# Score matmuls over both batches of a K pair, a mask matmul, and one matmul to turn P, in a two-layer decode kernel

## The chip, the cores and the metric

The kernel runs on one core of a Trainium2 chip. The metric is device time in microseconds, as the median of several runs; lower is better. A core has five engines that run their own instruction streams and meet at semaphores: TensorE (PE, matmuls; its weight loads appear as PEld), VectorE (DVE), ScalarE (ACT), GpSimd (POOL) and SyncE (SP, which here only issues transfers). Matmuls write to PSUM, eight banks of 512 float32 columns on 128 partitions; everything else lies in SBUF.

## What is computed

Two layers of a decode step for four sequences of one token each, with the same weights and the same K and V caches in both layers:

```python
x = x + attn(layernorm(x))    # wq, K cache, V cache, wo
x = x + glu(layernorm(x))     # wg, wu, wd
x = x + attn(layernorm(x))
x = x + glu(layernorm(x))
# attn: q = x @ wq                                  32 query heads, 8 KV heads, Dh = 128
#       scores = q . k * Dh**-0.5  over the last 2048 cached keys
#       o = softmax(scores) @ v;  return o @ wo
# glu:  (sigmoid(x @ wg) * (x @ wu)) @ wd            D = 512, F = 1792
```

There are B = 4 batches; four query heads share one KV head (REP = 4). Everything is bf16 with float32 sums.

## The kernel before

**Loads.** K of all eight KV heads stays in SBUF: it is loaded once, in the first layer, into slots of its own. A K pair (`load_k`, line 432) is the K of one head for two batches, 1 MB: partition 2p + i holds 32 consecutive keys of batch i of the pair, p = 0 to 63. V, wo, wq, wg, wu and wd go through a pool of nine 1 MB tiles (`_SlotPool`), which grows in the second layer, when a head's K is no longer needed. V is loaded in the same pair layout, once in each layer; one V tile is stashed in PSUM banks 0 to 3 between the layers. All loads are issued by SP in one order (line 385); a load that needs a tile waits until the last reader of that tile is done.

**Order of the work.** The program is a list of operations with what they read and write. `_schedule` (line 86) simulates it with rough costs (`_TM`, line 263) and picks the order of each engine's instructions; `_assign_sync` puts in the waits. An engine then runs its list strictly in that order. An operation's cost in the list is therefore no time, but it can change the order.

**Attention.** A unit is one KV head in one layer; there are eight in each layer. `attn` (line 829) keeps two units in flight, in buffers k2 = 0 and 1: the scores and statistics of unit u + 2 come before P times V of unit u, and the turning of P of unit u + 2 comes after it.

- `k_transpose` (line 685, first layer only): four 32x32-block transposes on DVE, each over 128 x 1024 float32, in place. Afterwards a partition is (block a of 32 old partitions, pair of head dimensions), and along the partition lie j (key within the old partition), c (half of the head), k = 2x + i (old partition within the block: x, and batch i of the pair) and t (even or odd dimension).
- `q_unit` (line 669): q of the unit's four heads is spread by four small matmuls into a block form, so that a matmul over 128 partitions gives the four blocks a separate rows; ACT copies it to `qbd`.
- `softmax_unit` (line 694): the scores are sixteen matmuls (line 708). For each cp = (c, t), four, and each batch b, four, the weights are 16 columns (a, query head r) of `qbd` and the moving operand is 512 keys of batch b alone, (j 32, x 16): every second k, four bf16 elements (8 bytes) apart. The four batches go to four column tiles, 32 partitions apart in one PSUM bank; 16 of each 32 rows are written. DVE then takes the maximum over 512 columns (line 716), adds a mask and the row maximum (`mk`, line 719), and takes the negated maximum over the four blocks by a transposing reduction (line 722). ACT computes exp with that as bias and sums each row (line 725), into the single buffer `prow`.
- `turn_p` (line 731): four matmuls with the permutation `perm` bring P's rows to their places for P times V: 64 rows of P at a time, 256 columns each, into two PSUM banks (line 737). ACT copies both banks to `prow`, interleaving them (line 742); DVE transposes 32x32 blocks into `ebuf` (line 746). The row sums are split in three bf16 parts on POOL (lines 750 to 754), summed over partitions by three matmuls (line 760) and inverted (line 767).
- `pv_unit` (line 770): for each V tile, 32 matmuls with 128 x 128 of V as weights and 8 columns of P (line 781), then normalization (line 789), a permutation (line 799) and a masking (line 804); `wo_unit` (line 811): 16 matmuls with wo (line 820).

**Setup.** `perm`, `sel_f`, `sel_b`, `sel_r` and `maskr` (lines 522 to 560) are built once on POOL and DVE. The two score banks are zeroed once (line 521), and the part of a bank that unit 8 uses instead, since the stash fills bank 0, is zeroed by `zero_q` (line 664). Query projections are at lines 629 to 665, the GLU at 865 to 977.

## Time and profile before

Seven runs: median 188.09 us, 187.28 to 189.4. The profile is of one further execution.

| | |
|---|---|
| profiled execution, its own time | 188.77 us |
| its span | 186.9 us |
| PE busy | 111.5 us (60%), 2016 matmuls |
| PE weight loads busy | 62.1 us (33%), 2016 |
| DVE busy | 90.5 us (48%), 209 |
| ACT busy | 31.2 us (17%) |
| POOL busy | 15.2 us (8%) |
| DMA | 72.12 MB, mean 386 GB/s |
| mean granted clock of PE | 0.708 |
| score matmuls, line 708 | 256, 32.3 us busy, mean 632 ns |
| turn of P, line 737 | 64, 7.1 us busy, mean 305 ns |
| copy of turned P, line 742 | 16, 9.4 us, mean 586 ns |
| row maximum, line 716 | 16, 10.9 us, mean 683 ns |

Where the stages lie: first projection to 15 us, first attention to 107, first GLU to 119, second projection to 130, second attention 126 to 175, last GLU to 186.

How to read it: busy times add up what an engine spent in instructions, while matmuls overlap (four column tiles run side by side), so PE's busy time is not a measure of its rate. A group's row gives its line, engine, operation, output and inputs with shapes, count, busy time and mean, and then the idle time just before it with what ended most of that. "issue" stands for time in which the engine waited for nothing that the profile shows. The granted clock is 0.50 or 1.00 of full speed in any moment.

### The profile page before, as it was taken

To read this page: it belongs to the slowest core of one execution; us is meant where nothing else is said; L and a number is where in the kernel's file an instruction comes from. 1 tells how busy PE (TensorE), PEld (TensorE's weight loads), DVE (VectorE), ACT (ScalarE), POOL (GpSimd) and SP (SyncE) were. 2 spreads that over 40 slices of the span, in tenths; PEclk is the share of its full clock that TensorE was granted. 3 is DMA by queue.
4 is the path that set the end of the run, shared out by engine and by line. 5 is a ranking of instruction groups with operands and counts; after the bars stand their busy time and mean duration, and the time that the engine had idled before them with its cause. 6 is when DMAs were issued, how large, how long until landed. Compare 5 with 4: busy or idle time off the path is not lost.

```text
span 186.9 us, 4539 instructions
## 1 busy us (share of the span) xinstructions
PE 111.5 (60%) x2016; PEld 62.1 (33%) x2016; DVE 90.5 (48%) x209; ACT 31.2 (17%) x78; POOL 15.2 (8%) x79
## 2 busy tenths in 40 slices
PE   1544541744637164460855474449989989985685
PEld 0011110332404133040435332212255655485342
DVE  6209998355763838539322542226634442340340
ACT  2002011510303003020020010001364211320010
POOL 5000010210101001010010000000113110110000
PEclk9999998755857655585575555555998796785557
DMA  5999999999999999999999999999999999999800
GB/s 199 422 422 431 421 415 416 426 417 419 413 423 419 421 422 411 420 421 421 414 417 419 401 406 414 370 375 421 363 401 428 424 415 419 415 404 411 323 32 1
DMA packets 12307, 72.12 MB, mean 386 GB/s; under 512 B 1144, under 2 KB 1152, under 8 KB 5632
## 3 DMA queue, kind: packets, MB, share of 16 engines
q1 hardware_dynamic: 12280, 71.84, 94.0%
q8 instruction: 15, 0.25, 0.5%
q14 instruction: 4, 0.03, 0.0%
q10 hardware_dynamic: 8, 0.00, 0.0%
HBM read 71.83 MB, written 0.00 MB: 384 GB/s over the span
## 4 chain that ended last, share of the span: by engine, by line
DMA 47%; PE 31%; DVE 8%; SPq 6%; issue 3%; ACT 2%; ACTq 0%
DMA arena<-in_A_v_cache_dram 24%; DMA arena<-in_A_k_cache_dram 14%; PE ps L708 10%; PE ps L781 8%; SPq L385 6%; DMA arena<-in_A_wq_dram 5%; DMA arena<-in_B_w_up_dram 5%; DVE arena L689 2%; PE ps L882 2%; PE ps L820 2%; PE ps L737 2%; PE ps L940 2%; PE ps L641 2%; DVE ps L494 1%; DVE nmax L716 1%
## 5 line engine op out<-in xcount | busy, mean ns | idle before, releaser
L781 PE MATMUL ps<-ebuf,arena 128*128 128x8 bf16 x1024 | 31.6, 167 | 21.7 <-DMA arena<-in_A_v_cache_dram 18.4
L708 PE MATMUL ps<-arena,qbd 128*16 128x512 bf16 x256 | 32.3, 632 | 17.7 <-DVE arena L689 17.3
L689 DVE STREAM_TRANSPOSE arena<-arena 128x1024 f32<-128x1024 f32 x32 | 37.8, 1215 | 1.7 <-DMA arena<-in_A_k_cache_dram 1.3
L781 PEld LDWEIGHTS ps<-ebuf,arena 128*128 128x128 bf16 x1024 | 28.8, 100 | 28.4 <-DMA arena<-in_A_v_cache_dram 24.4
L716 DVE TENSOR_REDUCE nmax<-ps 128x1 f32<-128x512 f32 x16 | 10.9, 683 | 23.4 <-PE ps L708 23.4
L725 ACT ACTIVATE prow<-ps,nmax 128x512 bf16<-128x512 f32 x16 | 11.0, 687 | 42.6 <-DVE nmax L722 29.4
L708 PEld LDWEIGHTS ps<-arena,qbd 128*16 128x16 bf16 x256 | 6.3, 99 | 31.0 <-DVE arena L689 17.9
L750 POOL CAST s<-psm 128x1 bf16<-128x1 f32 x16 | 3.0, 187 | 146.0 <-ACT prow L725 146.0
L682 ACT CAST qbd<-ps 128x256 bf16<-128x256 f32 x16 | 6.0, 372 | 42.9 <-PE ps L708 34.0
L641 PE MATMUL ps<-arena,xn 128*4 128x512 bf16 x64 | 8.3, 601 | 8.1 <-DMA arena<-in_A_wq_dram 8.1
L789 DVE TENSOR_TENSOR onb<-ps,rinv 128x16 bf16<-128x16 f32 x16 | 2.9, 182 | 20.3 <-PE ps L781 20.3
L742 ACT CAST prow<-ps 128x512 bf16<-128x512 f32 x16 | 9.4, 586 | 10.2 <-PE ps L737 10.0
L746 DVE STREAM_TRANSPOSE ebuf<-prow 128x256 f32<-128x256 f32 x16 | 7.0, 436 | 7.5 <-ACT prow L742 7.5
L820 PE MATMUL ps<-onp,arena 128*128 128x16 bf16 x256 | 9.3, 173 | 1.8 <-DVE onp L804 1.0
L820 PEld LDWEIGHTS ps<-onp,arena 128*128 128x128 bf16 x256 | 7.9, 101 | 4.4 <-issue 3.6
L618 ACT ACTIVATE lnv<-ps 128x4 f32<-128x4 f32 x4 | 0.7, 174 | 51.2 <-PE ps L614 51.2
L652 DVE STREAM_TRANSPOSE ebuf<-ps 128x512 f32<-128x512 f32 x4 | 2.9, 717 | 12.9 <-PE ps L641 12.8
L737 PE MATMUL ps<-prow,perm 64*128 64x256 bf16 x64 | 7.1, 305 | 3.1 <-ACT prow L725 3.1
L882 PE MATMUL ps<-arena,xn 128*4 128x448 bf16 x64 | 6.8, 564 | 2.4 <-DMA arena<-in_B_w_up_dram 1.7
L677 PE MATMUL ps<-qh,eyew 32*128 32x64 bf16 x64 | 5.6, 216 | 3.4 <-ACT qbd L682 1.9
L677 PEld LDWEIGHTS ps<-qh,eyew 32*128 32x128 bf16 x64 | 3.3, 105 | 9.3 <-ACT qbd L682 4.0
L804 DVE TENSOR_TENSOR onp<-ps,maskp 128x64 bf16<-128x64 f32 x16 | 3.5, 220 | 5.9 <-PE ps L799 5.8
(71 smaller groups left out, 85.9 us busy)
## 6 DMA issues: line engine op xcount, KB each, us to landing
arena<-in_A_v_cache_dram SPq DMA_DIRECT2D x30, 1024.0 KB, 20.9
arena<-in_A_k_cache_dram SPq DMA_DIRECT2D x16, 1024.0 KB, 25.0
arena<-in_A_wq_dram SPq DMA_DIRECT2D x8, 1024.0 KB, 9.1
arena<-in_A_wo_dram SPq DMA_DIRECT2D x4, 1024.0 KB, 25.5
arena<-in_B_w_gate_dram SPq DMA_DIRECT2D x4, 896.0 KB, 18.0
arena<-in_B_w_up_dram SPq DMA_DIRECT2D x4, 896.0 KB, 16.1
arena<-in_B_w_down_dram SPq DMA_DIRECT2D x2, 1024.0 KB, 13.2
arena<-in_B_w_down_dram SPq DMA_DIRECT2D x1, 768.0 KB, 7.4
```

The lines of the kernel that those rows point to most:

```text
L385: o = P.op("sync", name, 0.0, lambda e, dst=dst, src=src: e.dma_start(dst, src), r=r, w=w, dma_bytes=nbytes, dma_rate=tm[rate])
L641: last = pe.matmul(ps[32 * hh:32 * hh + NB, qb, :], xn[:, c * NB:(c + 1) * NB], tile_ap(s)[:, o + hh * 512:o + (hh + 1) * 512], start=(c = ...
L677: last = pe.matmul(dst[:, :, :, a * REP:(a + 1) * REP], eyew[32 * hh:32 * hh + 32, 96 - 32 * a:224 - 32 * a], src, start=True, stop=True)
L689: P.op("vector", "T%d_%d" % (h, t), c_dve(1024), lambda v, v32=v32: v.transpose(v32, v32), r=[("slot", 4 * h + t)], w=[("slot", 4 * h + t)])
L708: last = pe.matmul(ps[32 * gi:32 * gi + NR, bank, :], qbd[:, q0:q0 + NR], kt[:, cp // 2, cp % 2, b % 2, :, :], start=(cp == 0), stop=(cp = ...
L716: lambda v: v.tensor_reduce(nmax[:, k2:k2 + 1], ps[:, bank, :], AXX, ALU.max),
L725: lambda a: a.activation(prow[:, :].rearrange("p (m x t) -> p m x t", x=16, t=2), ps[:, bank, :].rearrange("p (m t x) -> p m x t", x=16, t ...
L737: last = pe.matmul(ps[:, PBS[i], 0:256], perm[64 * i:64 * i + 64, jh * 128:(jh + 1) * 128], prow[64 * i:64 * i + 64, jh * 256:(jh + 1) * 2 ...
L742: lambda a: a.copy(prow[:, :].rearrange("p (y i t) -> p i y t", i=2, t=2), ps[:, PBS[0]:PBS[0] + 2, 0:256].rearrange("p i (y t) -> p i y t ...
L781: last = pe.matmul(ps[:, ob, bp * 8:bp * 8 + 8], src[:, j * 128:(j + 1) * 128], ev[:, j % 2, j % 16 // 2, x0:x0 + 8], start=(j == 0), stop ...
L820: last = pe.matmul(ps[:, WB, c * NR:(c + 1) * NR], tile_ap(s)[:, o + r_ * D + c * 128:o + r_ * D + (c + 1) * 128], ov[:, r_ * NR:(r_ + 1) ...
L882: last = pe.matmul(ps[32 * g:32 * g + NB, OBS[n], 0:NF], xn[:, c * NB:(c + 1) * NB], tile_ap(s)[:, o:o + NF], start=(c == 0), stop=(c == N ...
```

## The change

Keys are no longer split by batch for the scores. A score matmul now takes 512 neighbouring keys of a K pair, both batches mixed (16 values of j, all 32 of k, two bf16 elements or 4 bytes apart), and 32 columns of weights (batch i, block a, head r). The four column tiles are now (half jh of j, pair bp). A score of a query against a key of the other batch is thus computed too. It is ruled out by a matmul with start=True ahead of the others, which writes -1e30 where row's and key's batch differ and 0 elsewhere: weights `msk_s` (128 x 32, two rows not zero), moving operand `msk_m`, two columns repeated 256 times. There are 20 matmuls for the scores in place of 16, and all 128 rows of the bank are written, so both zeroings go.

A batch's keys are now in two column tiles, 64 partitions apart. So two DVE copies of 64 x 1 exchange the row maxima between the halves, and `mk` takes the larger of both. P's turn is one matmul 128 x 128 by 512 into one bank, which depends on k2, and the copy to `prow` is straight. `perm`, `sel_r` and `maskr` have the new row order, q's block form is built in the order (c, b, r), and the setup has eight smaller selections for `perm` in place of four, and three operations for the masks.

```diff
-        P.op("vector", "zero_s", 1100.0, lambda v: v.memset(ps[:, 0:2, :], 0.0), w=[("s0",)], banks=SB)
...
         for jh in range(2):
             for bp in range(2):
-                P.op("gpsimd", "perm%d_%d" % (jh, bp), 300.0,
...
+                for i in range(2):
+                    z0 = 16 * jh + 8 * bp + REP * i
+                    P.op("gpsimd", "perm%d_%d_%d" % (jh, bp, i), 200.0,
...
+        P.op("gpsimd", "msk_s", 200.0,
+             lambda g: g.affine_select(msk_s[:, :].rearrange("p (i y) -> p i y", i=2),
+                                       ones_f[:, :].rearrange("p (i y) -> p i y", i=2),
+                                       [[1, 2], [0, NR]], ALU.is_equal, 0.0, base=-1, channel_multiplier=1),
+             r=[("ones_f",)], w=[("msk_s",)])
+        P.op("vector", "msk_s2", 100.0, lambda v: v.tensor_scalar(msk_s[:, :], msk_s[:, :], -1.0e30, None, ALU.mult),
+             r=[("msk_s",)], w=[("msk_s",)])
+        P.op("gpsimd", "msk_m", 200.0,
+             lambda g: g.affine_select(msk_m[:, :], ones_f[:, 0:2], [[-1, 2]], ALU.is_equal, 0.0, base=0, channel_multiplier=1),
+             r=[("ones_f",)], w=[("msk_m",)])
...
-                    P.op("vector", "zero_q", c_dve(160), lambda v, qb=qb: v.memset(ps[:, qb, 0:160], 0.0), r=[("qh", i)], w=[("pss", 2)], banks=(qb,))
...
+                for gi in range(4):
+                    last = pe.matmul(ps[32 * gi:32 * gi + 32, bank, :], msk_s[:, :],
+                                     msk_m[:, :].unsqueeze(1).broadcast_to([128, 256, 2]), start=True, stop=False)
                 for cp in range(4):
-                    for b in range(NB):
-                        gi = 2 * (b % 2) + b // 2
-                        kt = kpair(hk, b // 2).rearrange("p (j c x i t) -> p c t i j x", c=2, x=16, i=2, t=2)
-                        q0 = ((k2 * NB + b) * 4 + cp) * NR
-                        last = pe.matmul(ps[32 * gi:32 * gi + NR, bank, :], qbd[:, q0:q0 + NR],
-                                         kt[:, cp // 2, cp % 2, b % 2, :, :], start=(cp == 0), stop=(cp == 3))
+                    for gi in range(4):
+                        jh, bp = gi // 2, gi % 2
+                        kt = kpair(hk, bp).rearrange("p (j c k t) -> p c t j k", c=2, k=32, t=2)
+                        q0 = ((k2 * 4 + cp) * 2 + bp) * 32
+                        last = pe.matmul(ps[32 * gi:32 * gi + 32, bank, :], qbd[:, q0:q0 + 32],
+                                         kt[:, cp // 2, cp % 2, jh * NJ:(jh + 1) * NJ, :], start=False, stop=(cp == 3))
                 return last
-            P.op("tensor", "S" + tag, 16 * tm["pe_row"], e_s,
+            P.op("tensor", "S" + tag, 20 * tm["pe_row"], e_s,
...
+            for g in range(2):
+                P.op("vector", "nx%d%s" % (g, tag), tm["dve_small"],
+                     lambda v, g=g: v.tensor_copy(nmax[64 * g:64 * g + 64, 4 + k2:5 + k2],
+                                                  nmax[64 - 64 * g:128 - 64 * g, k2:k2 + 1]),
+                     r=[("mx", k2)], w=[("nx", k2, g)])
             P.op("vector", "mk" + tag, tm["dve_small"],
-                 lambda v: v.tensor_scalar(mk, maskr[:, :], nmax[:, k2:k2 + 1], None, ALU.add),
-                 r=[("mx", k2), ("maskr",)], w=[("mk", k2)])
+                 lambda v: v.scalar_tensor_tensor(mk, nmax[:, 4 + k2:5 + k2].broadcast_to([128, 32]), nmax[:, k2:k2 + 1],
+                                                  maskr[:, :], ALU.max, ALU.add),
+                 r=[("mx", k2), ("nx", k2, 0), ("nx", k2, 1), ("maskr",)], w=[("mk", k2)])
...
-            def e_pp(pe):
-                last = None
-                for jh in range(2):
-                    for i in range(2):
-                        last = pe.matmul(ps[:, PBS[i], 0:256], perm[64 * i:64 * i + 64, jh * 128:(jh + 1) * 128],
-                                         prow[64 * i:64 * i + 64, jh * 256:(jh + 1) * 256], start=(jh == 0), stop=(jh == 1))
-                return last
-            P.op("tensor", "pp" + tag, tm["pe_sq"], e_pp, r=[("prow",)] + perms, w=[("ppb",)], banks=PBS)
-            P.op("scalar", "pc" + tag, c_act(512),
-                 lambda a: a.copy(prow[:, :].rearrange("p (y i t) -> p i y t", i=2, t=2),
-                                  ps[:, PBS[0]:PBS[0] + 2, 0:256].rearrange("p i (y t) -> p i y t", t=2)),
-                 r=[("ppb",)], w=[("prow",)], banks=PBS)
+            P.op("tensor", "pp" + tag, tm["pe_sq"],
+                 lambda pe: pe.matmul(ps[:, PBS[k2], :], perm[:, :], prow[:, :], start=True, stop=True),
+                 r=[("prow",)] + perms, w=[("ppb", k2)], banks=(PBS[k2],))
+            P.op("scalar", "pc" + tag, c_act(512), lambda a: a.copy(prow[:, :], ps[:, PBS[k2], :]),
+                 r=[("ppb", k2)], w=[("prow",)], banks=(PBS[k2],))
```

## The prediction

> **What bounds the kernel now.** I read the page first (slices, groups), then the timeline of the second attention layer, then busy time by stretch with the granted clock, then the chain of waits.
>
> ```profile
> DMA  5999999999999999999999999999999999999800
> ...
> L708 PE MATMUL ps<-arena,qbd 128*16 128x512 bf16 x256 | 32.3, 632 | 17.7 <-DVE arena L689 17.3
> ...
> L737 PE MATMUL ps<-prow,perm 64*128 64x256 bf16 x64 | 7.1, 305 | 3.1 <-ACT prow L725 3.1
> ```
>
> The DMA engines are full until about 177 us. That decides the time up to about 126 us: first attention, first GLU and second query projection all end on a transfer (wq for the second layer is waited for until 123.58). From 126 us the chain of waits names no transfer: the weights of the last GLU are there when it asks. It is PE almost throughout, and the end is 12 us of short serial work behind attention. So only what changes between 126 and 174 us counts in full.
>
> Inside that stage the timeline shows something the groups hide:
>
> ```profile
> 153.14 0.17 PE L820 MATMUL ps<-onp,arena 128*128 128x16 bf16 x1 [0.79 <-issue]
> ...
> 159.38 0.55 PE L781 MATMUL ps<-ebuf,arena 128*128 128x8 bf16 x16 [0.35 <-issue]
> ...
> 171.72 0.17 PE L781 MATMUL ps<-ebuf,arena 128*128 128x8 bf16 x1 [2.22 <-issue]
> ```
>
> These pauses cut groups in the middle (15 of 16, 16 of 32, 31 of 32 matmuls), so no semaphore explains them. Counting matmuls by start, the pauses end at numbers 1494, 1622, 1749 and 1875: every 128 matmuls, which with their 128 weight loads are 256 instructions. The page has 15 packets on the queue "instruction", 0.25 MB, 16 KB each. The packet list has them at 150.7, 156.8, 163.0 and 169.2 us, about 3.6 us after PE enters a block, 1.0 us long; the next block opens 1.4 us later. So a block lasts max(its execution, 6.0 to 6.35 us): 146.8, 153.1, 159.4, 165.7, 171.7 us. Before that, blocks were bound by execution (133.4, 141.6, 146.8).
>
> The score matmuls do not follow the clock:
>
> ```profile
> core 0: us, PE busy (x) PEld busy (x) DVE busy (x) ACT busy (x) POOL busy (x), PEclk, DMA share, GB/s
> 45.00:48.00 3.00, 3.00 (x56) 1.41 (x53) 0.52 (x1) 0.37 (x1) 0.00 (x0) 0.50 0.98 407
> ...
> 139.00:141.20 2.20, 2.20 (x27) 0.55 (x25) 0.56 (x4) 0.87 (x3) 0.76 (x4) 1.00 1.03 428
> ```
> ```profile
> 45.36 2.08 PE L708 MATMUL ps<-arena,qbd 128*16 128x512 bf16 x16
> ...
> 139.04 2.02 PE L708 MATMUL ps<-arena,qbd 128*16 128x512 bf16 x16
> ```
>
> At clock 0.50 and at 1.00 the sixteen take 2.0 us; their four rounds of four column tiles start 413 to 472 ns apart in every unit, mean about 448.
>
> **The skill.** "TensorE: Matmul & The Clock Gate", Back-to-back issue gap, gives N/1.2 ns cold and N/2.4 + 2.5 ns warm: 427 and 216 ns for 512 columns. The trace agrees on contiguous reads when cold (L882, 448 columns, rounds 373 ns apart) but the warm figure is not reached by the scores. "SBUF — State Buffer", Specifications (TRN2), says lines of 16 bytes need two hits each for full bandwidth. The scores read at a stride of 8 bytes, just two hits, and still stay at the slow rate; four tiles at once seem to need more. "Runtime: NRT & Kernel Launch", Instruction fetch mechanics, says instructions come in 16 KiB blocks of 256 and the crossing is "mostly hidden"; the block size agrees, the hiding does not (2.22 us). "VectorE: DVE Perf Modes", Two Vector instructions with no wait between them, says that an instruction whose quadrant differs from the last is held until those before it end; no row of before isolates that.
>
> **The change, part by part.** All counts are per unit (head and layer, 16 units, 8 of them after 126 us).
>
> 1. Scores. Sixteen matmuls with 16 columns of weights become four mask matmuls plus sixteen with 32 columns: five rounds instead of four. Columns streamed per matmul stay 512. The unknown is the rate, since keys are now read at a stride of 4 bytes instead of 8. Upper bound: no faster, one more round of 0.45 us, +0.45. Lower bound: the full clock when granted, 4 x 0.216 + 0.379 for the last (213 ns of streaming and 166 ns beyond it, as 64x256 L737 shows: 274 minus 107) = 1.24 us, -0.75; when the clock is 0.50, 5 rounds at 427 plus 0.2 = 2.33, +0.33. For the full rate speaks that the contiguous projection at 129.47 ends 0.08 us earlier than its cold twin at 126.41 because the clock rises during its second round. Against it: no row reads four tiles at stride 4. I take +0.45, the only rate that this read pattern's nearest row has shown, and keep both ends.
>
> 2. Turning P. Four matmuls 64x256 become one 128x512. They ran two at a time: 0.39 us warm, 0.60 cold in the timeline; one of 512 columns is 213 + 166 = 0.38 warm, 427 + 205 (a cold L737 row is 417, less 213) = 0.63 cold. Nothing gained. The copy (L742, 586 ns) moves the same 512 elements: nothing. One bank instead of two frees nobody, since the single prow orders the units.
>
> 3. Softmax statistics. Two copies nx are put between the maximum (L716) and mk (L719). The chain of waits prices the steps around:
>
> ```profile
> 69.88 0.70 DVE nmax L716
> 70.58 0.02 issue
> 70.60 0.25 DVE mxt L719
> 70.85 0.02 issue
> 70.88 0.22 DVE nmax L722
> 71.10 0.02 issue
> ```
>
> A small DVE row takes 174 ns (L862, L576), so with gaps two held copies cost 0.4 us; pipelined 0.27, and below 0.2 nothing excludes. I take 0.4 and keep 0.2 to 0.45. mk with two inputs costs what the scalar form does, about 0.22 (L903 is 218). How much is seen: the wait ahead of a turn of P is covered by PV and WO. In the timeline exp with its accumulator ends 0.27, 0.18, 0.24 and 0.44 us before L737 starts in the closest four units (137.75, 143.67, 148.41, 161.11), over 0.8 us in the others. So 0.13 + 0.22 + 0.16 = 0.5 us is seen, of which 0.35 before 147. If the planner puts other DVE work between the copies the cover is gone, and each step waits for a whole instruction, up to 0.7 us here.
>
> 4. Setup. The 0.91 us memset of two score banks (L521) and the one of 0.19 at 126.03 go; four perm instructions become eight of about 0.3, two masks and a DVE multiply are added on POOL and DVE before 20 us. sel_f waits for all eight and holds the small DVE steps behind it, up to 1.5 us. The first projections wait for wq (PE idles 1.42 to 1.47 us before each later chunk), and the last chunk comes at 13.13: nothing. The 0.19 lies beside PE's projection: nothing. qc and qx change order of elements, not counts: nothing.
>
> 5. First layer. Eight units grow by 0.45 on PE and 0.4 on DVE. PE and DVE have idle time there: V is waited for by up to 4.9 us (L781), and DVE needs 7.1 + 0.4 us a unit (four L689 of 1.215 and the rows behind them) against 11 us of transfers (2 MB of K, 2 of V, half a MB of wo at 418 GB/s). SP waits for slots that PE frees, but a transfer lands 20.9 us after its issue (V, median), so a release 1 us later meets a full queue. Nothing. In the second layer the last w_down pieces are issued by 163.9 and used at 181.6; 2.5 us later is still in time.
>
> 6. Instruction count: +8 -6 = +2 a unit, 16 matmuls by the end. Block borders come 16 matmuls (0.47 us) earlier in the work: cancels where execution bounds, costs 0.47 where fetching does.
>
> **Sum.** Up to 147 us execution bounds PE: five score groups, 5 x 0.45 = 2.25, plus 0.35 of chain = 2.6. After that a block's execution grows from 5.35 to 5.35 + 1.14 x (0.45 + 0.2) = 6.1 us, about what fetching allows anyway, so the remaining 1.35 us of growth takes the place of the pauses of 0.79, 0.35 and 0.6; the 2.22 stays. I take off 0.2 for mask rounds at the full clock (same two elements over and over). +2.4 us: span 186.9 to 189.3. The profiled run took 188.77, 1.9 over its span and 0.7 over the median; I put the difference on the median: 188.09 + 2.4 = 190.5.
>
> **Rivals.**
> *Full rate, gain fetched away (chance 0.30, 188.2 us).* Stride 4 streams at the granted clock. Warm scores save 0.75, cold ones lose 0.33. The clock follows the streaming: it fell to 0.50 at 154.1, 160.9 and 167.7, after stretches with few scores, so shorter scores make it colder, and about half would be cold. By 141.6 I get 2 x 0.33 - 2 x 0.75 = -0.8. From there every block takes 6.2, where 141.6 to 146.8 now takes 5.13: five blocks end at 140.8 + 31 = 171.8, plus 0.47 of displaced work. +0.1 to +0.5, range 187.3 to 189.2. Speaks for it: the projection at 129.47. Against: it needs a rate nobody shows.
> *Other side: faster (0.12, 186.6).* The same full rate, and fetching keeps the 4.9 us of the block entered at 141.6 (its packet came 2.6 us after, at 144.2) instead of 6.2. Two blocks like that would save 2.6, less displaced work and 0.6 of chain: -1.5. It decides once fetched blocks average below about 5.8 us; the last four at 6.0 to 6.35 speak against it.
> *The chain becomes the limit (0.16, 192.0).* DVE's two steps get others' work between them, or P's turn comes to stand ahead of PV in PE's order, so that 0.3 more is seen in the five units whose growth no pause covers: 2.4 + 1.5 = +3.9. For it: PE is in order and slack is 0.18 to 0.44. Against: the planner counts the copies.
> That one matmul for P brings nothing is in all of them.
>
> **Numbers.** Same rate and a fifth round, 0.42, 190.5 (189.3 to 191.8). About 0.5% (0.9 us) is what a measurement can tell: below 187.15 faster, above 189.03 slower. Faster: 0.10 of the fast case and 0.03 of the fetched-away one = 0.13. Same: 0.21 of the fetched-away case, 0.02 of the likeliest and 0.02 of the fast one = 0.25. Slower: 0.62. The range 187.0 to 192.0 leaves out most of the fast rival and half of the last one, 0.2.
>
> **What would show it.** L708: twenty matmuls, 2.45 us a unit whatever the clock (right), or 1.3 in stretches of clock 1.00 (rival). L737's successor: one row near 0.38 to 0.63. DVE: two rows of about 0.17 behind L716. PE pauses by "issue" in mid-group still 128 matmuls apart, shorter except the last. DMA full to 177 us, last attention matmul 2.4 us later. Wrong if the stage before 126 us moves, or if the scores speed up and the pauses shrink.

## The result, and the profile after

The changed kernel takes 189.22 us in the median of 24 runs (187.83 to 190.76), the kernel before 187.77 in 59 runs. The ratio is 1.0077, with a 95% interval of 1.0056 to 1.0097: slower by about 1.4 us. Measured once more beside the first experiments, the same kernel gave 1.0046 (1.0017 to 1.0074), 0.9 us. One run differs from the next by a microsecond or more, so only medians are compared below, and every time is set against the kernel before on the same chip.

The profiled execution of the changed kernel (188.68 us, span 185.9) happens to be shorter than the one shown of before (188.77, span 186.9). One row of the last GLU is enough to account for that. These are its lines in the timeline of PE, first of the kernel before, then of the kernel after (start, duration, engine and line, operation, count, and the idle time ahead):

```profile
181.58 3.15 PE L940 MATMUL ps<-arena,hT 128*4 128x256 bf16 x28 [0.63 <-DVE hT L909]
```
```profile
181.93 1.82 PE L951 MATMUL ps<-arena,hT 128*4 128x256 bf16 x28 [0.63 <-DVE hT L920]
```

The same 28 matmuls ran at a granted clock of 0.50 in one and almost wholly at 1.00 in the other; in the repeat of the changed kernel they took 3.15 us again. That is 1.3 us that no edit made. A single span cannot show a change of this size; the medians can. The kernel itself repeats only to about half of it: its two measurements, 1.4 and 0.9 us, differ by 0.6 us as ratios.

The groups of the page after that answer to those shown of before (the turn of P, now line 752, is mostly missing from the trace and has no row there):

```profile
DMA  5999999999999999999999999999899999999930
...
L720 PE MATMUL ps<-arena,qbd 128*32 128x512 bf16 x256 | 29.2, 595 | 0.0
...
L713 PE MATMUL ps<-msk_m,msk_s 128*32 128x512 bf16 x64 | 9.8, 567 | 15.6 <-DVE arena L698 13.2
```

The transfers are as full as before. The stretch up to the second attention is unmoved: the last projection matmul ahead of the first scores of the second layer (the 24th of the 32 of that query projection) starts at 127.21 us (126.89 in the repeat) where it was 126.80. "The stage" is from here on the time from the start of that matmul to the start of the last wo matmul. It is 47.7 us in the trace before, 47.6 and 47.4 in the two traces after: the parts of the stage changed a good deal, but these single traces do not show the 1.4 us of the medians. The score groups in the timeline of the changed kernel:

```profile
131.03 0.39 PE L713 MATMUL ps<-msk_m,msk_s 128*32 128x512 bf16 x4
131.25 1.11 PE L720 MATMUL ps<-arena,qbd 128*32 128x512 bf16 x16
...
144.71 0.62 PE L713 MATMUL ps<-msk_m,msk_s 128*32 128x512 bf16 x4 [0.79 <-ACT prow L743]
145.11 1.92 PE L720 MATMUL ps<-arena,qbd 128*32 128x512 bf16 x16
```

Twenty matmuls now take 1.33 us in the unit at 131 us (131.03 to 132.36), where the clock is 1.00, and 2.32 us in the unit at 144.7, where it is 0.50. Sixteen took 2.0 us before, at either clock. By the start times of the matmuls, a round of four column tiles takes 220 to 246 ns at clock 1.00 and about 427 at 0.50; before it took 413 to 472 at both. So the rounds follow the granted clock at a step of 4 bytes, and at a step of 8 bytes they do not.

But the clock itself is lower. These are busy times by stretch, over the same 43 us of the second attention, first before, then after; the column behind POOL is the mean granted clock:

```profile
132.00:175.00 43.00, 37.04 (x852) 23.68 (x848) 15.65 (x57) 12.80 (x30) 6.34 (x33) 0.80 1.01 409
```
```profile
132.00:175.00 43.00, 35.50 (x849) 24.73 (x848) 18.37 (x73) 12.62 (x30) 6.34 (x33) 0.69 1.00 402
```

In the stage, the clock stood at 1.00 for 27.3 us before and for 17.1 us after. (In the traces of the kernel after, the first 3.4 to 3.8 us of the stage have no clock record; the rounds there take 427 ns.) Judged by their rounds, five of the eight score groups of that layer ran wholly at 0.50.

And PE now waits for exp, the step of ACT that the turn of P needs. The waits of PE in that layer, each with its total, number and longest, first before, then the repeat of after:

```profile
PE ps L781 <- issue: 2.6, 2, 2.2
...
PE ps L820 <- issue: 0.8, 1, 0.8
```
```profile
PE ps L752 <- ACT prow L743: 2.0, 5, 0.9
...
PE ps L792 <- issue: 1.2, 1, 1.2
...
PE ps L713 <- issue: 0.4, 1, 0.4
```

Before, the largest of these sums are pauses put down to issue, in the middle of groups, and none is for exp. After, the turn of P waits for exp five times, 2.0 us in all, and the pauses at issue have shrunk from 3.4 to 1.6 us. That these pauses are instruction fetching is what the runs with cut loads, below, speak for.

One thing more changed: the order of PE's work. The score operation's cost in the list grew from 16 to 20 rows, and the planner placed the sixth score group of this layer later. Before, it follows a turn of P directly; after, the next unit's q, P times V and wo matmuls come first:

```profile
148.41 0.39 PE L737 MATMUL ps<-prow,perm 64*128 64x256 bf16 x4
148.74 2.00 PE L708 MATMUL ps<-arena,qbd 128*16 128x512 bf16 x16
```
```profile
151.64 0.57 PE L831 MATMUL ps<-onp,arena 128*128 128x16 bf16 x16
152.15 1.14 PE L713 MATMUL ps<-msk_m,msk_s 128*32 128x512 bf16 x4
```

In this layer all versions of the kernel after have the new order, and so has b_mask; b_group, b_nx and b_light have the old one. What the order is worth by itself was not measured.

### The profile page after: what moved, and what is told of

Read it like the earlier page. It is cut to its first block, busy times and chain, and to the rows that moved or that the text cites. A ratio compares the mean times of both kernels' runs of the same rounds, so it can differ in the third digit from the quotient of the medians.

```text
span 185.9 us, 4596 instructions
## 1 busy us (share of the span) xinstructions
PE 109.2 (59%) x2018; PEld 65.4 (35%) x2032; DVE 93.4 (50%) x240; ACT 31.1 (17%) x78; POOL 15.9 (9%) x85
## 4 chain that ended last, share of the span: by engine, by line
DMA 47%; PE 25%; DVE 13%; SPq 6%; ACT 4%; issue 3%; ACTq 0%
DMA arena<-in_A_v_cache_dram 23%; DMA arena<-in_A_k_cache_dram 14%; PE ps L720 9%; SPq L387 6%; DMA arena<-in_A_wq_dram 5%; DMA arena<-in_B_w_up_dram 5%; PE ps L792 4%; DVE arena L698 3%; PE ps L713 3%; DVE nmax L728 3%; ACT prow L743 3%; PE ps L893 2%; PE ps L651 2%; DVE ps L496 1%; PE ps L831 1%
## 5 line engine op out<-in xcount | busy, mean ns | idle before, releaser
L792 PEld LDWEIGHTS ps<-ebuf,arena 128*128 128x128 bf16 x1024 | 29.8, 102 | 25.6 <-DMA arena<-in_A_v_cache_dram 22.2
L698 DVE STREAM_TRANSPOSE arena<-arena 128x1024 f32<-128x1024 f32 x32 | 38.0, 1215 | 1.0 <-DMA arena<-in_A_k_cache_dram 0.9
L720 PE MATMUL ps<-arena,qbd 128*32 128x512 bf16 x256 | 29.2, 595 | 0.0
L713 PE MATMUL ps<-msk_m,msk_s 128*32 128x512 bf16 x64 | 9.8, 567 | 15.6 <-DVE arena L698 13.2
L720 PEld LDWEIGHTS ps<-arena,qbd 128*32 128x32 bf16 x256 | 9.1, 131 | 12.0 <-issue 11.1
L713 PEld LDWEIGHTS ps<-msk_m,msk_s 128*32 128x32 bf16 x64 | 1.9, 100 | 16.5 <-DVE arena L698 10.2
L810 PE MATMUL ps<-onb,permo 128*128 128x16 bf16 x64 | 4.3, 177 | 3.6 <-DVE onb L800 3.6
```

The source lines that it names most:

```text
L698: P.op("vector", "T%d_%d" % (h, t), c_dve(1024), lambda v, v32=v32: v.transpose(v32, v32), r=[("slot", 4 * h + t)], w=[("slot", 4 * h + t)])
L713: last = pe.matmul(ps[32 * gi:32 * gi + 32, bank, :], msk_s[:, :], msk_m[:, :].unsqueeze(1).broadcast_to([128, 256, 2]), start=True, stop= ...
L720: last = pe.matmul(ps[32 * gi:32 * gi + 32, bank, :], qbd[:, q0:q0 + 32], kt[:, cp // 2, cp % 2, jh * NJ:(jh + 1) * NJ, :], start=False, s ...
L792: last = pe.matmul(ps[:, ob, bp * 8:bp * 8 + 8], src[:, j * 128:(j + 1) * 128], ev[:, j % 2, j % 16 // 2, x0:x0 + 8], start=(j == 0), stop ...
```

## The experiments

Three explanations stood against each other (theories 1 to 3 of the first expectations). *Parts*: the mask round and the exchange of maxima each cost their own time on PE's path, and the faster reading gives some back. *Fetch*: blocks of 256 PE instructions arrive at a limited pace, so what is saved or added inside a block is evened out by pauses. *Clock*: what streams faster is granted less clock.

**The change again, and without one part each.** The first run is the kernel after, unchanged. In the second, the two copies nx go, and `mk` takes a half's own maximum, so the maxima of the two halves are not exchanged. In the third, the mask round goes, so the other batch's keys are not ruled out.

a_no_nx:

```diff
-            for g in range(2):
-                P.op("vector", "nx%d%s" % (g, tag), tm["dve_small"],
...
-                 lambda v: v.scalar_tensor_tensor(mk, nmax[:, 4 + k2:5 + k2].broadcast_to([128, 32]), nmax[:, k2:k2 + 1],
+                 lambda v: v.scalar_tensor_tensor(mk, nmax[:, k2:k2 + 1].broadcast_to([128, 32]), nmax[:, k2:k2 + 1],
```

a_no_mask:

```diff
-                for gi in range(4):
-                    last = pe.matmul(ps[32 * gi:32 * gi + 32, bank, :], msk_s[:, :],
-                                     msk_m[:, :].unsqueeze(1).broadcast_to([128, 256, 2]), start=True, stop=False)
...
-                                         kt[:, cp // 2, cp % 2, jh * NJ:(jh + 1) * NJ, :], start=False, stop=(cp == 3))
+                                         kt[:, cp // 2, cp % 2, jh * NJ:(jh + 1) * NJ, :], start=(cp == 0), stop=(cp == 3))
```

> The changed kernel as it is. It should repeat 1.4 us over the kernel before (0.9 to 1.9). Its second trace tells what in the first was luck: the last GLU's matmuls ran 1.3 us faster there because the clock rose at 182 us.

> The changed kernel without the exchange of row maxima between the halves of the partitions (this part of the computation is left out; mk takes the own maximum twice). Theory 1, PE waits for the longer chain of statistics: the after trace has PE idle 0.42 to 0.79 us behind exp before five turns of P, so 1.2 to 2.4 us less than the changed kernel, that is, at or below the kernel before. Theory 2, instruction blocks set the pace of the second attention: within 0.5 us of the changed kernel.

> The changed kernel without the mask matmuls (scores against the other batch's keys then stay in: this part is left out). Theory 1: the fifth round is 0.43 us at clock 0.50 and 0.22 at 1.00, eight units, of which PE waits for other things in some: 1 to 2.5 us less than the changed kernel. Theory 2, instruction blocks: within 0.5 us of it. Theory 3, the clock: less streaming lowers the granted clock further, and of 2.5 us under 1 is seen.

Measured: a_again 188.77 us, 1.0046. a_no_nx 187.76, 0.999 (0.9964 to 1.0017). a_no_mask 187.96, 1.001 (0.9987 to 1.0033). So, against a_again, the exchange is worth about 1.0 us and the mask round about 0.8, each give or take 0.7; against the first measurement each would be 0.6 more. Without either one the kernel stands level with the kernel before. Fetching alone (within 0.5) fits neither well; the exchange is worth less than *parts* had it (1.2 to 2.4), and the mask round what *clock* had (under 1). In a_no_nx the time from the start of the row maximum to the start of exp is 1.32 us in each of the last four units, as in the kernel before (1.31); with the copies it is 1.68 to 1.84. That is 0.4 to 0.5 us a unit for two copies of 0.33 us together. The chain of the kernel after shows such a unit:

```profile
147.08 0.69 DVE nmax L728
147.77 0.14 DVE onp L815
147.93 0.15 DVE nmax L732
148.11 0.16 DVE nmax L732
148.30 0.26 DVE mxt L736
148.58 0.22 DVE nmax L740
148.84 0.05 issue
148.89 0.79 ACT prow L743 x2
149.68 0.58 issue
150.26 0.39 PE ps L686 x4
```

Each step waits for the end of the one before, and another unit's step (`onp`) stands in between. In the unit before, at 142 us, the chain holds a transpose of `ebuf` too, 0.45 us between the copies and `mk`. The 0.58 us of "issue" at the end is where the turn of P, missing from the trace, belongs.

**Without both parts.** The kernel after without exchange and without mask round; left are the new reading, the turn of P by one matmul and the new order.

```diff
-                for gi in range(4):
-                    last = pe.matmul(ps[32 * gi:32 * gi + 32, bank, :], msk_s[:, :],
...
-            for g in range(2):
-                P.op("vector", "nx%d%s" % (g, tag), tm["dve_small"],
...
```

> The kernel after without the exchange of maxima and without the mask round (the output is then not the reference's): what is left of the change is the faster reading and the turn of P by one matmul. If the costs of the two parts add up (1.0 and 0.8 us), 187.0, that is 0.9 us below the kernel before. If both were paid out of one wait, that of PE for exp, or if shorter streaming lets the clock fall, about 187.7 to 188.0, as each of them alone gave.

Measured: 187.15 us, 0.9962 (0.994 to 0.9984). It is 0.7 us below the kernel before and 1.6 below a_again: within the noise, the costs of the two parts add up. What is left of the change is a small gain, and PE's timeline shows why it isn't a larger one. These groups of P times V are cut in the middle, by pauses put down to issue:

```profile
146.84 0.51 PE L784 MATMUL ps<-ebuf,arena 128*128 128x8 bf16 x13 [0.52 <-issue]
...
159.28 0.46 PE L784 MATMUL ps<-ebuf,arena 128*128 128x8 bf16 x11 [0.45 <-issue]
...
165.41 0.83 PE L784 MATMUL ps<-ebuf,arena 128*128 128x8 bf16 x25 [0.27 <-issue]
...
171.94 0.19 PE L784 MATMUL ps<-ebuf,arena 128*128 128x8 bf16 x1 [2.93 <-issue]
```

They come to 4.2 us, against 3.4 before and 1.6 after: here PE has less to do and stands still longer. (Pauses of 0.37 us ahead of whole score groups in this trace are not counted: there a turn of P, which takes 0.39 us or more, is missing from the records.) The clock was at 1.00 for only 6.8 us of this stage.

**The step of the reading alone, from both sides.** In a_stride8 the changed kernel reads its 512 columns in another order, all keys of one batch, then all of the other, 8 bytes apart. The mask's two columns are repeated in the same new order. (P's columns then no longer fit V's keys.) In b_group the kernel before reads at 4 bytes: its K transposes write each batch's keys side by side, and sixteen score matmuls with 16 columns of weights remain, without mask or exchange.

a_stride8:

```diff
-                                     msk_m[:, :].unsqueeze(1).broadcast_to([128, 256, 2]), start=True, stop=False)
+                                     msk_m[:, :].unsqueeze(1).unsqueeze(3).broadcast_to([128, 16, 2, 16]), start=True, stop=False)
...
-                        kt = kpair(hk, bp).rearrange("p (j c k t) -> p c t j k", c=2, k=32, t=2)
+                        kt = kpair(hk, bp).rearrange("p (j c x i t) -> p c t j i x", c=2, x=16, i=2, t=2)
```

b_group:

```diff
-                 P.op("vector", "T%d_%d" % (h, t), c_dve(1024), lambda v, v32=v32: v.transpose(v32, v32),
+                 P.op("vector", "T%d_%d" % (h, t), c_dve(1024), lambda v, v32=v32: v.transpose(
+                          v32.rearrange("p (n i x) -> p n x i", i=2, x=16), v32),
...
-                        kt = kpair(hk, b // 2).rearrange("p (j c x i t) -> p c t i j x", c=2, x=16, i=2, t=2)
+                        kt = kpair(hk, b // 2).rearrange("p (j c i x t) -> p c t i j x", c=2, x=16, i=2, t=2)
```

> The kernel after, with the 512 columns of each score matmul read in another order: all keys of batch 0 of a K pair, then all of batch 1, 16 neighbours each, so that the step is 8 bytes again as in the kernel before; number of matmuls, mask round, exchange of maxima and the turn of P stay. (The columns of P then come in another order than the keys of V, so the output is not the reference's.) In the trace of the kernel after, a round of four score matmuls took 427 ns at clock 0.50 and 220 to 246 ns at 1.00. Both theories expect about 440 to 460 ns at clock 1.00 here, as in the kernel before, and 427 to 450 at 0.50. Theory A, that the faster reading shortens the path wherever the clock is 1.00: three units of the second layer ran there, 4 rounds x 0.22 us each, so +2.0 to +2.7 us, 190.8 to 191.5. Theory B, that a faster reading mostly lets the clock fall sooner or is waited away behind exp: 0 to +0.8 us, 188.8 to 189.6, with clearly more than 17 us of the second attention at clock 1.00.

> The kernel before with one thing changed: the transposes of K write the keys of each batch next to each other, so that the sixteen score matmuls of the kernel before read at a stride of 4 bytes instead of 8, with no mask, no exchange and P turned as before. If the stride sets the rate: rounds of 0.22 us at clock 1.00 and 0.43 at 0.50, scores of 1.05 or 1.9 us instead of 2.0. Theory 1: 1 to 2.5 us faster than the kernel before. Theory 2, instruction blocks: within 0.5 us of it, with longer pauses in mid-group. If stride is not the cause: rounds stay at 0.45.

Measured: a_stride8 190.14 us, 1.0126 (1.0082 to 1.0171), 1.4 us above a_again. Its rounds take 414 to 475 ns at either clock, and the score group of the unit at 131 us shows it, first in a_stride8, then in a_again, both at clock 1.00:

```profile
130.78 1.99 PE L720 MATMUL ps<-arena,qbd 128*32 128x512 bf16 x16
```
```profile
130.71 1.12 PE L720 MATMUL ps<-arena,qbd 128*32 128x512 bf16 x16
```

So the step alone sets the rate: the mask rounds of the same trace, which read two columns over and over, take 226 ns at clock 1.00. The faster reading is worth about 1.4 us, give or take 1.0, between the two theories (0.9 against the first measurement). The clock stood at 1.00 for 27.3 us of the stage with 8 bytes, as in the kernel before, and for 17.1 with 4.

The two traces also part the waits for exp, for PE's order is the same in both. The longest one, in a_again, comes right behind two units read at full clock. In a_stride8 that exp ends at 134.9 us, but PE is still at the third unit's scores until 135.6, and nothing is waited for. First a_again, then a_stride8:

```profile
134.71 0.39 PE L752 MATMUL ps<-prow,perm 128*128 128x512 bf16 x1 [0.87 <-ACT prow L743]
```
```profile
133.67 1.97 PE L720 MATMUL ps<-arena,qbd 128*32 128x512 bf16 x16
...
169.13 0.96 PE L792 MATMUL ps<-ebuf,arena 128*128 128x8 bf16 x32 [0.69 <-ACT prow L743]
```

The later waits are there at 8 bytes as well: PE stands idle for 0.23, 0.15, 0.37 and 0.40 us up to the end of exp in four of the last five units of a_stride8. (The turn that follows is missing from this trace, so the 0.69 in the row above is 0.40 and a turn.) In a_again it is 0.10, 0.19, 0.18, 0.06 and 0.42 in the last five. So, in these traces, the first wait comes from the faster reading, and the later ones do not.

b_group took 193.7 us, 1.0313 (1.0285 to 1.0341), for a reason that no theory named. The groups of its page:

```profile
L689 DVE STREAM_TRANSPOSE arena<-arena 128x1024 f32<-128x1024 f32 x32 | 57.1, 1865 | 0.0
L709 PE MATMUL ps<-arena,qbd 128*16 128x512 bf16 x256 | 28.8, 594 | 44.4 <-DVE arena L689 33.8
```

A transpose with the permuted output takes 1865 ns where the plain one takes 1215. Thirty-two of them add 20.8 us on DVE. These transposes are 29% of the chain that ended last, where they were 2%, and the stage begins at 133.49 us in place of 126.80. The stage itself is shorter, 46.3 us against 47.7 (one trace each), and its rounds took 216 to 226 ns at clock 1.00. That agrees in size with a_stride8. It is also why neighbouring keys of one batch, which would need neither mask nor exchange, can't be had for nothing in this way.

**One part alone, in the kernel before.** In b_nx the exchange is put into the old softmax chain. In b_mask a fifth round, with zero weights, stands ahead of the old scores; its operation has the cost of 20 rows, so PE's order is the new one.

b_nx:

```diff
+            for g in range(2):
+                P.op("vector", "nx%d%s" % (g, tag), tm["dve_small"],
...
```

b_mask:

```diff
+                for gi in range(4):
+                    last = pe.matmul(ps[32 * gi:32 * gi + NR, bank, :], msk_z[:, :],
+                                     msk_z[:, 0:2].unsqueeze(1).broadcast_to([128, 256, 2]), start=True, stop=False)
...
-                                         kt[:, cp // 2, cp % 2, b % 2, :, :], start=(cp == 0), stop=(cp == 3))
+                                         kt[:, cp // 2, cp % 2, b % 2, :, :], start=False, stop=(cp == 3))
```

> The kernel before with the two exchange copies of row maxima added to its softmax chain (and the row mask made with the larger of both maxima, which changes no result). The copies took 0.33 us a unit in the kernel after. Theory A, that PE waits for exp in the second layer and each unit pays: leaving them out of the kernel after saved 1.0 us, so +0.8 to +1.2, 188.7 to 189.1. Theory B, that the kernel before has slack behind exp, since its scores come later by the pauses of PE: 0 to +0.4, 187.9 to 188.3. The exp-ended idle time of PE in the second layer tells which.

> The kernel before with a fifth round of matmuls with zero weights ahead of the scores of each unit, as the mask round of the kernel after (20 matmuls in place of 16, no change of result). Leaving the mask round out of the kernel after saved 0.8 us. Theory A, that a round is paid at its streaming time (427 ns at clock 0.50, about 215 at 1.00) in the five to six units that PE's order carries: +1.2 to +2.2 us, 189.1 to 190.1. Theory B, that part of it only fills pauses and waits: +0.5 to +1.0, 188.4 to 188.9. Theory C, that the longer streaming keeps the clock at 1.00 for longer and pays for the round: 187.4 to 188.1, with more than 27 us of the second attention at clock 1.00.

Measured: b_nx 188.25 us, 1.0017 (0.9995 to 1.0039): some 0.3 us (-0.1 to 0.7), not 1.0. The chain grows there too, to 1.7 to 1.8 us from maximum to exp in the last four units, but the only wait for exp that PE's timeline shows after 140 us is this one:

```profile
149.83 0.39 PE L743 MATMUL ps<-prow,perm 64*128 64x256 bf16 x4 [0.25 <-ACT prow L731]
```

So the kernel before had slack for most of the growth. The same copies cost more in the changed kernel (1.0 us against its repeat, 1.6 against the first measurement).

b_mask 190.89 us, 1.0164 (1.0109 to 1.0219): 3.0 us, more than any theory had; the lower end of the interval, 2.0 us, is inside the first. Its extra round takes 0.22 us in six units and about 0.4 in two, 2.1 us in all. What the other 0.9 us are is open: the traced execution, 189.65 us, is 1.2 below the median, the noise is as large, and PE's order differs from that of the kernel before. The clock was at 1.00 for 34.1 us of the stage, the most of all kernels here, and that did not pay for the round, as the third theory had it: at a step of 8 bytes the scores don't use it.

**Without the fetch pauses.** In the second layer V's loads are cut to 256 elements of each partition, in the kernel before and in the kernel after, so that the transfers hardly compete with the fetching of instructions. V's old contents are multiplied.

```diff
-            load(("V", h, bp, k), n_use, "bw_8k", (2 * SLOT, pair_d(A_v, h, bp), True))
+            src = pair_d(A_v, h, bp)
+            load(("V", h, bp, k), n_use, "bw_8k", (2 * SLOT, src, True) if k == 0 else (256, src[:, :, 0:256], True))
```

> The kernel before with the V loads of the second layer cut to the first 256 elements of each partition (the output is then not the reference's; V's old contents are multiplied instead). From about 126 us on the transfers then hardly compete with the instruction fetches of PE. Fetch theory: the pauses that the trace puts down to issue in the second attention (0.79, 0.35 and 2.22 us in the kernel before) go to under 0.6 us in sum, the time from the last query projection to the last wo matmul falls from 47.7 us by 2.5 to 3.5 us, to 44.2 to 45.2. Rival: the pauses have another cause (PE's own sequencer), and the stage keeps 47 to 48 us and its pauses.

> The kernel after with the same cut of the second layer's V loads. Fetch theory: its pauses (0.43 and 1.17 us) go, its waits for exp stay or grow, the stage falls from 47.4 us by 1.0 to 2.0 us, to 45.4 to 46.4, and the changed kernel is then clearly behind the one before under the same cut, by 1 to 2 us in that stage, since the pauses no longer level the two. Rival: both keep their pauses and stand within 0.5 us of each other, as in the profiles of the uncut kernels.

Measured: b_light 183.2 us, 0.9774 (0.9729 to 0.9818). a_light 185.51, 0.9863 (0.9817 to 0.9908). Neither has a pause at issue among PE's waits in the stage. It falls from 47.7 to 43.0 us in the kernel before and from 47.4 (the repeat) to 45.2 in the kernel after. Both falls are larger than the pauses that went (3.4 and 1.6 us), so the cut does something more, and what is open. With it, the changed kernel is behind by 2.2 us in this stage, and by 1.7 (ratios) to 2.3 us (medians) in all, where it is behind by 0.9 to 1.4 in the full kernels. With four runs of each, the 1.7 is uncertain by 1.2, so that the gap is wider without the pauses is likely, not shown. The packets of the instruction queue agree with fetching as the cause of the pauses: in b_light they come at 161.3, 165.4 and 168.9 us, 4.1 and 3.5 apart, where the kernels before and after have 5.9 to 6.6 in this part of the stage. Here are PE's waits in a_light; b_light has none for exp.

```profile
PE ps L753 <- ACT prow L744: 2.0, 5, 0.8
```

The two traces also give an account of the 2.2 us. Summed over the eight units, from the first to the last start of a unit's sixteen score matmuls, the reading is 2.5 us shorter than in b_light (8.6 against 11.1). The mask rounds take 2.8 us (0.23 to 0.43 each). The waits for exp are 2.0 us: 0.83 at 134.9 us, right behind two units read at full clock, whose gain is thus partly waited away; the other 1.1 in four later units, which is about what leaving out the exchange saved. Together +2.3. The later waits fit the slack: in b_light exp ends 0.06 to 0.28 us ahead of the turn of P in the last five units, less than the 0.4 to 0.5 us by which the exchange lengthens the chain.

**A version meant to beat both.** The mask round needs neither q nor K. In a_early_fold it is issued ahead of the turn of P of the unit before, where PE waits for exp, and the rest of PE's order stays. The exchange is folded into `mk`: two operations on 64 partitions, each reading the other half's maxima, in place of two copies and one operation.

```diff
+        for so, e_m in early:
+            m = _Op(len(P.ops), "tensor", "M" + so.name, 0.0, e_m)
...
+            pe_order.insert(i, m)
...
+                P.op("vector", "mk%d%s" % (g, tag), tm["dve_small"],
+                     lambda v, g=g: v.scalar_tensor_tensor(
+                         mk[64 * g:64 * g + 64, :], nmax[64 - 64 * g:128 - 64 * g, k2:k2 + 1].broadcast_to([64, 32]),
+                         nmax[64 * g:64 * g + 64, k2:k2 + 1], maskr[64 * g:64 * g + 64, :], ALU.max, ALU.add),
```

> The kernel after with the mask round of a unit moved ahead of the matmul that turns P of the unit before it, where PE waits for exp, all else in the same order; and with the exchange of maxima folded into the row mask (two operations on 64 partitions, each reading the maxima of the other half, in place of two copies and one operation). Chain theory: the exp-ended idle time of PE in the second layer (0.87 + 0.15 + 0.25 + 0.23 + 0.47 us in a_again) takes in most of the mask rounds, worth 0.4 to 0.9 us, and the shorter chain is worth 0.3 to 0.6: 187.4 to 188.1, level with the kernel before or below it. Fetch theory: what is saved comes back as pauses at issue, since the number of instructions stays: 188.2 to 188.7.

> The early mask round and folded exchange, with the V loads of the second layer cut as in b_light and a_light (the output is then not the reference's). In the uncut pair of kernels the exp-ended waits of PE fell from about 2.0 to 1.0 us and the time hardly moved. Fetch theory: the pauses at issue took the gain; without them it shows, so 184.4 to 184.9 against 185.5 of a_light, with no pause at issue over 0.2 us. Clock theory: PE, streaming more evenly, is granted full speed for less of the stage (10.2 us against 17.1 in the uncut pair), and its rounds take the gain back: 185.2 to 185.8.

Measured: 188.38 us, 1.0038 (1.0012 to 1.0064). It is slower than the kernel before, and not told apart from the changed one. The waits for exp fell to 1.0 us as meant, and the mid-group pause at the end is again there:

```profile
PE ps L760 <- ACT prow L751: 1.0, 2, 0.8
PE ps L729 <- issue: 0.9, 1, 0.9
PE ps L800 <- issue: 0.9, 1, 0.9
```

(The first of the two pauses stands between two groups, the second inside one; no turn of P is missing from this trace.) Folding brought almost nothing: two operations of 247 ns, 0.49 us, in place of 0.33 + 0.23. a_early_light, the same with the cut loads, took 185.68 us, 0.9862 (0.982 to 0.9904), level with a_light. So the fetch theory finds no support in this version: without pauses a gain from the early mask round is not seen either, though one of up to about 1 us would be lost in the noise. The clock theory's number was met (185.2 to 185.8), and its mechanism is in the trace: one unit that ran at clock 1.00 in a_light, scores and mask round in 1.34 us, ran at 0.50 here, 1.0 us longer, while the waits for exp fell from 2.0 to about 1.1 us (two turns of P, missing from the records, not counted in). With one trace of each this is an account, not a proof.

## Why the prediction was right or wrong

The time on record, 190.5 us, is 1.3 us above the median measured, inside its range and on the right side. As growth it is +2.4 on record against +1.4; the other 0.3 us is the seven-run median that it started from. The likeliest case is not what happened, so that the number came near is in part luck: terms were off in opposite directions. The prediction's own sign of being wrong came, too: the scores sped up and the pauses shrank.

*Step 1, the scores: wrong.* "+0.45 a unit, no faster at stride 4" failed. The lower bound written beside it is what the chip did: 1.33 us at clock 1.00, 2.3 at 0.50, so -0.7 and +0.3 us a unit against bounds of -0.75 and +0.33. The rival of the full rate had this right, and also that shorter scores make the clock colder: five of eight units ran wholly at 0.50. The nearest row was taken as evidence for a rate though it differed in just the thing that was changed, the step. Of the +2.25 us in the sum, the runs leave about +0.8 for the mask round and -1.4 for the reading, -0.6 in all. The change at the rate that the step assumed was run as well: a_stride8 is 2.3 us over the kernel before, where the sum has +2.4. Without the error in the rate, the rest of the sum holds as a whole; its parts were not measured at that step.

*Step 2, the turn of P: as far as seen, right.* The records that there are show 0.39 us warm and 0.61 cold for the one matmul, against 0.38 and 0.63 in the step. No run tested it by itself.

*Step 3, the chain: mechanism right, size too small.* The sum had 0.35 us; leaving out the exchange saved 1.0. The unit's growth was put at 0.4 and measured 0.4 to 0.5. The slack was read rightly for the old kernel as it stands, and b_nx agrees (0.3 us). But pauses of PE stood in it: 0.79, 0.35 and 0.61 us in three of the last four units before. Without them these units have 0.37, 0.09 and 0.24 us of slack instead of 1.16, 0.44 and 0.85 (the last pause is the 0.6 of the prediction), close to what b_light shows and less than the growth. In the new kernel the turn of P waits for exp in five places, 2.0 us. The first wait, 0.87 us, comes from the faster scores, which bring PE there sooner; a_stride8 does not have it. The other four, 1.1 us, stand in a_stride8 too, so they come from the longer chain and the lost cover, not from the reading; how much of that is PE's new order is open. The third rival, the chain as the limit, describes this better than the sum did, though its 192.0 us is too much: its first way, another unit's steps in the chain, is in the trace; its second, the turn ahead of P times V in PE's order, is not.

*Steps 4 and 5, setup and first layer: right.* The stage begins within 0.4 us of where it did.

*Step 6 and the pauses: right in kind.* The late blocks have pauses, which go when the loads are cut; the stage is then 4.7 and 2.2 us shorter. The sum let the growth replace the small pauses and kept the one of 2.22 us. It was 1.17 instead, so the last one gave way as well: the pauses shrank by 1.8 us in all.

*The sum.* With cut loads, and so without pauses, the change costs 1.7 to 2.3 us; in the full kernel it costs 0.9 to 1.4. That the smaller pauses give back the difference fits the traces; the runs are too few to show it. The sum had +2.4 with the pauses already counted. The rival with the gain fetched away, at 188.2, erred about as far on the other side: it had the rate right and the colder clock, and left out most of the chain.

## What to carry to other kernels

Price a faster read by the clock that it will be granted, not by the one in the old trace: here 4 bytes in place of 8 halved a round at clock 1.00, and only about a third of the stage was left at that clock. A chain that is just covered is not free to lengthen: count its slack without the pauses that happen to stand in it, and with the shorter work that the same edit brings. Where a planner picks the order, compare the order of the engine in both kernels before a difference is read as the price of the added part. And when pauses at issue stand in the path, take the transfers away in both kernels and compare again, with enough runs, since pauses can hide gains and losses alike.

## What was not expected of the hardware

- With four column tiles side by side, a round of 512 bf16 columns takes 220 to 246 ns at clock 1.00 with a step of 4 bytes and 414 to 475 ns with 8. The Trainium skill, "SBUF — State Buffer", Specifications (TRN2), asks for at least two hits on a 16-byte line for full bandwidth; 8 bytes have two and are slow here.
- The granted clock stood at 1.00 for longer where the reading was slower. It changes at intervals of about 3.4 us, which the Trainium skill, "TensorE: Matmul & The Clock Gate", Part 1: The HAM clock gate, names as its window. Time at clock 1.00 in the second attention: 34.1 us with an extra round at 8 bytes, 27.3 in each of the three other kernels with full loads that read at 8 bytes, 10.2 to 17.1 at 4 bytes with the mask round, 6.8 without it. What decides it was not found. PE's busy time alone does not: in a_no_mask PE is busy for 29.3 of the 30.7 us from 136.5 to 167.2 us (86% at the least in any interval of 3.4 us) and the clock stays at 0.50 throughout. Over the stretch shown above for before and after, a_no_mask has:

```profile
132.00:175.00 43.00, 36.12 (x820) 24.29 (x812) 17.61 (x71) 12.26 (x29) 6.38 (x33) 0.55 1.01 409
```

- Blocks of 256 PE instructions come every 5.9 to 6.6 us beside full transfers late in the stage of the kernels before and after, with pauses of PE; with few transfers they came 3.5 to 4.3 us apart at the end of the stage (b_light, a_light), without pauses.
- A transpose of 32x32 blocks on DVE costs 1865 ns with a permuted output of 4-byte elements against 1215 with the plain one, and a DVE operation on 64 partitions (247 ns) costs no less than one on 128 (235).
